# Value products of two attention steps issued together, from the start of the attention loop

## The chip, the core and the metric

The kernel runs on one core of a Trainium2 chip. The metric is the device time of one execution in microseconds (us). TensorE (PE, with its weight loads shown as PEld) multiplies matrices into PSUM, which has eight banks of 128 x 512 float32; ScalarE (ACT), VectorE (DVE) and GpSimd (POOL) work on tiles; SyncE (SP) issues DMAs. Each engine takes its instructions in the order in which the program lists them, and waits on semaphores of the others.

## The reference, cut to what matters

Two mixing layers over the same sequence length are added with a gate. The attention part, which the change touches, is a full softmax attention with 32 heads of 16 columns over 2048 positions:

```python
H = 32; Dh = D // H                      # D = 512, S = 2048
q, k, v = qkv[0], qkv[1], qkv[2]         # from x @ wqkv
scores = jnp.einsum("bhqd,bhkd->bhqk", q, k) * scale
p = _softmax(scores, axis=-1)
o = jnp.einsum("bhqk,bhkd->bhqd", p, v)
a = o.transpose(0, 2, 1, 3).reshape(B, S, D) @ wo
...
y = einsum("ts,bse->bte", dft_seq_re, a_) - einsum("ts,bse->bte", dft_seq_im, b_)
return g * a + (1 - g) * y
```

The other part multiplies with large Fourier matrices. Here it matters only because its products fill PE in the later part of the attention loop.

## The kernel before, in words

The 32 heads are 16 pairs (`NP`). For each pair the kernel needs the largest score of each query before it can take exponentials. It gets these from **scans**: a scan (`scan`, L126) multiplies 128 queries of both heads with 512 keys into one pair of PSUM banks, and one DVE reduction (L137) takes the maximum of each row. There are 64 scans to a head pair, 1024 in all. The first 725 are done beside the projections and the Fourier products, in an earlier phase; the other 299 are done one per step in the attention loop.

The **attention loop** (L991) has 512 steps. A step takes one head pair `p`, one half `h` of the queries (1024 of them) and one block `kb` of 128 keys; 16 steps make a half pass, 32 a head pair. A step issues on PE, in this order:

1. the wide scores (`qk_both`, L229): 512 queries of both heads, two matmuls into a pair of banks. ACT takes one wide exponential of 128 x 1024 (L234) into the tile `eb`;
2. a scan (`next_scan`, L979), while there are any left;
3. the narrow scores (`qk_single`, L237): the other 512 queries of both heads, into two of three single banks. ACT takes two narrow exponentials of 128 x 512 (L242) into the tiles `e`;
4. value products (`flush`, L974, which calls `pv`, L753): four matmuls of 128 x 17 by 512 columns for each step flushed, one to each 32-column strip of the array, which add into the accumulator bank `pvb`. The 17th column of the values is one, so that it sums the exponentials.

All score matmuls, the scans among them, have a contraction over at most 50 rows and come in twos, one head in the upper and one in the lower half of the array.

The list `pend` holds the steps whose exponentials are ordered but whose value products are not. Step 0 is appended, step 1 flushes it, and from then on the number that is flushed in a step is set by the line that the change touches (L1030).

The program is placed by hand: the order written is the order on each engine. PSUM is full: the scans have one pair of banks (`wide0`), the wide scores another (`wide1`), the narrow scores the three banks d0, d1 and k0 in turn, the accumulator the bank k1. In SBUF the wide exponentials have a ring of four tiles, the narrow ones rings of three and four.

When the last key block of a half pass has been flushed (`done[2] == NB - 1`), DVE copies the accumulator to `ob` (`quotients`, L762) and GpSimd fetches the sums from it; ten steps later `divide` (L771) takes reciprocals and scales. Queries and keys of the next pair are loaded by SP at fixed steps.

`MIX` is 301, the first step without a scan. From it on each step issues three pairs of matmuls of the Fourier part or the output product (`next(fill)`), ahead of the wide scores in even steps and between wide and narrow scores in odd ones, and value products are flushed two steps at a time, in even steps.

Of the kernel before, what the change touches and what calls it, by code (L numbers as in the profile page):

```python
# [46 lines left out]
MIX = TOTAL - FRONT + 1  # L47
# [6 lines left out]
def build(tc, xT, wqkv, wo, wrT, wiT, cr, ci, gate, out):  # L54
    nc = tc.nc
    with ExitStack() as ctx:
# [51 lines left out]
        def load_use(p):  # L108
            if p < NP:
                used[p], loads = row_loads(p, nc.sync)  # L110
                for load in loads:
                    load()
                qs, ks = used[p]
                for j in range(2):
                    b = 64 * j + 48
                    nc.sync.dma_start(ks[b:b + 2, :].bitcast(F32), ones_d)
                    for n in range(2):
                        nc.sync.dma_start(qs[b + n:b + n + 1, :].bitcast(F32),
                                          m_d[p][n:n + 1, :, j].rearrange("n g b k -> n b g k"))
# [610 lines left out]
        with ExitStack() as pa:  # L730
# [15 lines left out]
            def qk2(p, h, kb, c):  # L746
                if c == 0:
                    return qk_both(p, h, kb)
                n = turn1[0]
                turn1[0] += 1  # L750
                return qk_single(p, h, kb, [ring[n % len(ring)] for ring in single])
# [10 lines left out]
            def quotients(p, h):  # L762
                ob = ap.tile([P, 512], F32, tag="ob", name="ob", bufs=2)
                nc.vector.tensor_copy(ob, pvb)  # L764
                lc = sm.tile([P, 16], F32, tag="lc", name="lc")
                for n, (c, j, r) in enumerate(quads):
                    nc.gpsimd.dma_start(lc[32 * n:32 * n + 32, :],  # L767
                                        ob[r + DH:r + VC, :].rearrange("p (s e) -> p s e", e=16))
                return p, h, ob, lc

            def divide(p, h, ob, lc):  # L771

                nc.vector.reciprocal(lc, lc)  # L773
                nc.gpsimd.dma_start(r_d[p][h].rearrange("n (s e) -> (n s) e", e=16), lc)  # L774
                for n, (c, j, r) in enumerate(quads):
                    nc.gpsimd.dma_start(rb[r:r + DH, :], r_d[p][h][n:n + 1, :].to_broadcast([DH, 512]))
                nc.gpsimd.tensor_mul(ob, ob, rb)
                kept = p >= NP - 2
                if p == NP - 2:
                    oh, ol = block(28 + 2 * h), block(29 + 2 * h)  # L780
                else:
                    pool, *tags = (cw, "chi", "clo") if kept else (ap, "oh", "ol")
                    oh, ol = (pool.tile([P, 512], F32R, tag=tag, name=tag) for tag in tags)
                nc.gpsimd.tensor_copy(oh, ob)
                nc.gpsimd.tensor_sub(ol, ob, oh.bitcast(F32))
                if kept:
                    direct.setdefault(h, []).append((oh, ol))
                    return
                for i, s in enumerate((oh, ol)):
                    nc.gpsimd.dma_start(o_d[p // 4][i][h, :, p % 4], s.bitcast(F32))  # L790
# [38 lines left out]
            def output_rows(c):  # L829

                for f in range(ND - 1):
                    for i in range(2):
                        a = oc[c, f, i] = block((0, 18)[c % 2] + 2 * f + i)
                        src = o_d[f][i][c // 2, c % 2].rearrange("p (j r) s -> r (p j) s", j=2)
                        nc.sync.dma_start(a.bitcast(F32), src[0:DH])
# [10 lines left out]
            def load_y(c):  # L846
                y4 = stk.tile([P, 4, D], F32, tag="stk", name="y4")
                nc.sync.dma_start(y4, y_d[c])
                for t in range(4 * c, 4 * c + 4):
                    ys[t] = y4[:, t % 4, :]  # L850
# [8 lines left out]
            def load_unit():  # L859
                if units:  # L860
                    t, u = units.pop(0)
                    raw = ap.tile([P, D], F32, tag="craw", name="craw", bufs=2)
                    raws.append(raw.rearrange("p (c q) -> p c q", q=P))
                    nc.sync.dma_start(raws[-1], ci[t, :, u * CS:(u + 1) * CS, :])

            def split_unit():
                if raws:
                    raw = raws.pop(0)
                    hi, lo = (cw.tile([P, 512], F32R, tag=tag, name=tag).rearrange("p (c q) -> p c q", q=P)
                              for tag in ("chi", "clo"))  # L870
                    nc.vector.tensor_copy(hi, raw)  # L871
                    nc.vector.tensor_sub(lo, raw, hi.bitcast(F32))
                    parts.append((hi, lo))
# [85 lines left out]
            def part(t, *ks):  # L959

                if t not in groups:
                    if t in (3, 9):
                        ps = pair_banks()
                        groups[t] = ps[:, 0, :], ps[:, 1, :]
                    else:
                        groups[t] = bank2() if t == 8 else (bank(), pvb if t == 11 else bank())
                for k in ks:
                    mix_rest(t, groups[t], k, k == 0 or 7 < t < 11, k == 2)
# [3 lines left out]
            halves, halved, pend = [], [], []  # L972

            def flush():  # L974
                done = pend.pop(0)
                pv(*done)
                return done

            def next_scan():  # L979
                n = seen[0]  # L980
                if n >= TOTAL:
                    return
                if n % SCANS == SCANS - 10:
                    load_scan(n // SCANS + 1)
                scan(n, pair_banks())
                seen[0] += 1
                if seen[0] % SCANS == 0:
                    late.extend(shift(n // SCANS))

            late = []  # L990
            for step in range(NP * PERIODS):  # L991
                p, i = step // PERIODS, step % PERIODS
                h, kb = i // NB, i % NB
                now[0] = step
                if i == 18:
                    load_use(p + 1)
                if step in (MIX - 24, MIX - 20):
                    load_unit()
                if step == MIX - 12:
                    split_unit()  # L1000
                if OUT - 10 <= step < OUT - 4 or step >= OUT + 4:
                    next(operands, None)
                if step in (OUT - 12, OUT + 1):
                    output_rows(int(step > OUT))
                if step in (OUT - 25, (NP - 1) * PERIODS):
                    for c in range(2):
                        load_y(c + 2 * (step > OUT))
                if step >= MIX and step % 2 == 0:
                    next(fill)
                if step == 0:  # L1010
                    pend.append((p, h, kb, ahead[:2]))
                    continue
                es = ahead[2:] if step == 1 else [qk2(p, h, kb, 0)]
                if step == 1:
                    es.append(qk2(p, h, kb, 1))
                    flush()
                if late:
                    late.pop(0)()
                if step == 2:
                    es.append(qk2(p, h, kb, 1))  # L1020
                if step > 1:
                    next_scan()
                if step > 2:
                    es.append(qk2(p, h, kb, 1))
                if step >= MIX and step % 2:
                    next(fill)
                if step == NP * PERIODS - 1:
                    part(3, 0)
                done = None
                for _ in range(min(len(pend), 1) if step < MIX else 0 if step % 2 else 2):  # L1030
                    done = flush()
                if done and done[2] == NB - 1:
                    halved.append((step + (10 if done[0] < NP - 2 else 7 if done[0] < NP - 1 else 3), quotients(*done[:2])))
                if halved and halved[0][0] <= step:
                    p_, h_ = halved[0][1][:2]
                    divide(*halved.pop(0)[1])
                    if p_ == NP - 2:
                        output_rest(h_)
                pend.append((p, h, kb, es))
# [76 lines left out]
```

## Time and profile before

| what | value |
|---|---|
| median of three runs | 1726.87 us (1726.72 to 1727.06) |
| span of the profiled execution | 1725.2 us |
| instructions | 36082 |
| chain that ended last, by engine | PE 96%, DVE 2%, DMA 1%, issue 1% |
| chain, largest lines | value products L755 29%, Fourier and projection products L185 25%, attention scores L210 19% |
| granted TensorE clock, 40 slices | 9 tenths or more in every slice |
| wide exponential of step 3 begins | 670.9 us |
| wide exponential of step 301 begins | 1237.1 us |

The profiled execution has no time of its own beside its span. In the rows below, a line number is that of the listing. A row of a group names the line, the engine, the operation, the output tile and the inputs, the shapes and the count, then the busy time and the mean duration in ns of one, then the idle time of the engine ahead of them and what ended it. A row of the order of time begins with start and duration in us; neighbours of one kind are merged, and a bracket at the end holds the idle time ahead and what ended it. All value products are at L755, wide and narrow scores at L210, scans at L135. The ends of matmuls are modelled, so that a busy PE can be a waiting one; its weight loads carry the semaphore waits.

### The profile page before, as it was taken

Reading aid. Unit: us, or ns where it says so; the run is one execution under the profiler, and the core shown is the slowest. Engines: PE = TensorE matmul, PEld = TensorE weight load, DVE = VectorE, ACT = ScalarE, POOL = GpSimd, SP = SyncE. Lnnn points to the kernel's source line nnn. Section 1 sums busy time; section 2 is a strip of 40 time slices with the busy share of each in tenths; the row PEclk is TensorE's granted clock in tenths of the full one; section 3 lists DMA queues with packets and bytes.
Section 4 is the critical chain, followed back from the end, with each engine's and each line's share of the span. In section 5 each row is a group of like instructions: output and inputs, shape, how many; then the busy total and the mean of one; then the engine's idle time right before and its main releaser. Section 6 shows DMA issues by size and latency. Waiting matters only on the chain.

```text
span 1725.2 us, 36082 instructions
## 1 busy us (share of the span) xinstructions
PE 1713.5 (99%) x13680; PEld 1044.7 (61%) x13680; DVE 1089.1 (63%) x2059; ACT 1506.8 (87%) x2489; POOL 648.7 (38%) x770
## 2 busy tenths in 40 slices
PE   9999999999999999999999999999999999999998
PEld 7888888988888885333333333333455555555554
DVE  6898888999999996666666666666512212122333
ACT  6447889888888888999999999999988888888886
POOL 3672436655555762223233242322322322223222
PEclk9999999999999999999999999999999999999999
DMA  7783557534337663243323342351334244265712
GB/s 257 241 285 75 156 158 211 158 112 115 103 111 211 153 136 72 37 73 58 66 59 67 54 82 44 58 107 37 65 80 94 72 110 91 67 150 139 175 36 101
DMA packets 123710, 193.03 MB, mean 112 GB/s; under 512 B 54112, under 2 KB 56656, under 8 KB 116624
## 3 DMA queue, kind: packets, MB, share of 16 engines
q1 hardware_dynamic: 84464, 170.20, 37.7%
q0 software_dynamic: 38496, 19.47, 5.7%
q8 instruction: 107, 1.75, 0.4%
q10 hardware_dynamic: 576, 1.05, 0.2%
q14 instruction: 67, 0.55, 0.1%
HBM read 129.63 MB, written 61.61 MB: 111 GB/s over the span
## 4 chain that ended last, share of the span: by engine, by line
PE 96%; DVE 2%; DMA 1%; issue 1%; ACT 0%; SPq 0%; DVEq 0%; POOL 0%; ACTq 0%; POOLq 0%
PE pvb L755 29%; PE xy L185 25%; PE s L210 19%; PE s L185 9%; PE s L154 9%; PE s L135 5%; DVE fold L160 1%; DMA q_d<-eh 0%; DMA raws<-wqkv 0%; DMA ks<-kf_d 0%; PE s L554 0%; DVE y L853 0%; ACT fold L158 0%; DVE s L278 0%; DVE b L334 0%
## 5 line engine op out<-in xcount | busy, mean ns | idle before, releaser
L234 ACT ACTIVATE eb<-s 128x1024 f32<-128x1024 f32 x512 | 578.7, 1130 | 65.4 <-PE s L210 65.4
L242 ACT ACTIVATE e<-s 128x512 f32<-128x512 f32 x1022 | 608.9, 709 | 0.4 <-PE s L210 0.4
L137 DVE TENSOR_REDUCE mx<-s 128x2 f32<-128x1024 f32 x364 | 441.4, 1224 | 188.7 <-PE s L135 188.5
L755 PE MATMUL pvb<-eb,va 128*17 128x512 f32 x2052 | 513.0, 597 | 0.0
L755 PE MATMUL pvb<-e,va 128*17 128x512 f32 x2044 | 512.1, 597 | 0.0
L160 DVE CUSTOM_DVE_ANT_0 fold<-s,fold 128x512 f32<-128x512 f32 x660 | 443.9, 690 | 52.7 <-PE s L154 24.4
L158 ACT ACTIVATE fold<-s 128x512 f32<-128x512 f32 x660 | 389.9, 603 | 73.3 <-PE s L154 52.3
L210 PEld LDWEIGHTS s<-qs,ks 50*128 50x128 f32 x2048 | 214.9, 184 | 355.2 <-ACT eb L234 255.1
L210 PE MATMUL s<-qs,ks 50*128 50x512 f32 x2048 | 420.0, 434 | 0.0
L185 PE MATMUL xy<-b,c 64*128 64x512 f32 x2448 | 397.3, 392 | 0.3 <-ACT c L333 0.3
L154 PE MATMUL s<-ks,qs 48*128 48x512 f32 x1320 | 315.3, 405 | 1.6 <-DVE mx L160 1.0
L185 PEld LDWEIGHTS xy<-b,c 64*128 64x128 f32 x2448 | 283.9, 187 | 17.6 <-issue 1.0
L154 PEld LDWEIGHTS s<-ks,qs 48*128 48x128 f32 x1320 | 172.9, 184 | 47.0 <-DVE mx L160 12.5
L774 POOL DMA_DIRECT2D r_d<-lc x31 | 18.1, 583 | 456.4 <-DVE lc L773 456.4
L755 PEld LDWEIGHTS pvb<-eb,va 128*17 128x17 f32 x2052 | 70.5, 96 | 189.9 <-issue 182.7
L135 PE MATMUL s<-ks,qs 48*128 48x512 f32 x728 | 151.6, 394 | 0.7 <-DVE mx L137 0.7
L767 POOL DMA_DIRECT2D lc<-ob x124 | 62.9, 514 | 156.3 <-DVE ob L764 156.1
L185 PE MATMUL xy<-w,b 64*128 64x512 f32 x768 | 115.3, 392 | 0.0
L365 POOL TENSOR_TENSOR c<-craw,c 128x512 fp32r<-128x512 f32 x84 | 109.4, 1302 | 6.7
L185 PE MATMUL s<-b,chi 64*128 64x512 f32 x670 | 105.4, 391 | 0.0
L364 POOL CAST c<-craw 128x512 fp32r<-128x512 f32 x84 | 53.3, 635 | 125.1 <-PE xy L185 120.1
L871 DVE CAST chi<-craw 128x512 fp32r<-128x512 f32 x40 | 19.1, 477 | 111.4 <-PE s L185 99.3
(136 smaller groups left out, 1535.2 us busy)
## 6 DMA issues: line engine op xcount, KB each, us to landing
qs<-q_d SPq DMA_DIRECT2D x66, 256.0 KB
craw<-ci SPq DMA_DIRECT2D x64, 256.0 KB
craw<-cr SPq DMA_DIRECT2D x60, 256.0 KB
ks<-k_d SPq DMA_DIRECT2D x44, 256.0 KB
qs<-q_d SPq DMA_DIRECT2D x66, 128.0 KB
ab_d<-ab SPq DMA_DIRECT2D x32, 256.0 KB
y_d<-y SPq DMA_DIRECT2D x32, 256.0 KB
o_d<-oh POOLq DMA_DIRECT2D x28, 256.0 KB, 13.8
```

Of the source, the lines that this page charges most:

```text
L135: nc.tensor.matmul(ps[:, j, :], qs[b:b + 48, qb * P:(qb + 1) * P], ks[b:b + 48, c * 512:(c + 1) * 512], start=True, stop=True)
L137: nc.vector.tensor_reduce(mx[p][:, :, qb, c], ps, axis=AX.X, op=ALU.max)
L154: nc.tensor.matmul(ps, qs[b:b + 48, qb * P:(qb + 1) * P], ks[b:b + 48, c * 512:(c + 1) * 512], start=True, stop=True)
L158: nc.scalar.activation(fold[j], ps, AF.Relu)
L160: nc.vector.tensor_tensor_reduce(out=fold[j], in0=ps, in1=fold[j], scale=1.0, scalar=-3.0e38, op0=ALU.add, op1=ALU.max, accum_out=mx[p][:, ...
L185: nc.tensor.matmul(ps[j], lhs[r], rhs[r], start=first, stop=last)
L210: nc.tensor.matmul(pss[j], ks[b:b + 50, kb * P:(kb + 1) * P], qs[b:b + 50, q0:q0 + 512], start=True, stop=True)
L234: nc.scalar.activation(e, ps, AF.Exp, scale=SCALE)
L242: nc.scalar.activation(e[j], pss[j], AF.Exp, scale=SCALE)
L365: sub(lo, raw, hi.bitcast(F32))
L755: nc.tensor.matmul(pvb[r:r + VC, :], va[:, kb, 2 * p + j, :], es[c][j], start=kb == 0, stop=kb == NB - 1, tile_position=(0, r))
L767: nc.gpsimd.dma_start(lc[32 * n:32 * n + 32, :], ob[r + DH:r + VC, :].rearrange("p (s e) -> p s e", e=16))
```

## The change

The number of steps flushed no longer depends on the phase. Before, each step under 301 flushed one step if there was one; now odd steps flush none and even steps up to two, in the whole loop.

```diff
                 done = None
-                for _ in range(min(len(pend), 1) if step < MIX else 0 if step % 2 else 2):
+                for _ in range(0 if step % 2 else min(len(pend), 2)):
                     done = flush()
                 if done and done[2] == NB - 1:
```

Step 2 still flushes step 1 alone. From step 4 on, an even step flushes the two steps before it: step 4 flushes 2 and 3, step 300 flushes 298 and 299. The last key block of a half pass has an odd step number and was flushed in the even step behind it; it still is.

## The prediction

> **What bounds the kernel now.** I read the page's totals first, then the totals of two stretches (the attention loop with scans, and the loop after them), the groups of instructions of the first stretch, and last the order of time inside single steps.
>
> ```profile
> PE 1713.5 (99%) x13680; PEld 1044.7 (61%) x13680; DVE 1089.1 (63%) x2059; ACT 1506.8 (87%) x2489; POOL 648.7 (38%) x770
> ```
>
> ```profile
> 670.90:1237.00 566.10, 565.38 (x4174) 215.91 (x4176) 383.27 (x354) 565.38 (x895) 164.53 (x249) 1.00 0.33 61
> 1241.50:1650.00 408.50, 408.50 (x3351) 215.58 (x3349) 91.55 (x154) 360.60 (x554) 106.71 (x160) 1.00 0.46 110
> ```
>
> ```profile
> L242 ACT ACTIVATE e<-s 128x512 f32<-128x512 f32 x597 | 376.0, 776 | 0.4 <-PE s L210 0.4
> L234 ACT ACTIVATE eb<-s 128x1024 f32<-128x1024 f32 x298 | 357.4, 1199 | 0.3 <-PE s L210 0.3
> ...
> L137 DVE TENSOR_REDUCE mx<-s 128x2 f32<-128x1024 f32 x298 | 365.2, 1225 | 181.3 <-PE s L135 181.3
> L764 DVE COPY ob<-pvb 128x512 f32<-128x512 f32 x18 | 12.5, 692 | 1.5
> ```
>
> The columns of the stretches are the stretch, its length, the busy time of PE, PEld, DVE, ACT and POOL, the granted clock, the DMA share and GB/s. The first stretch runs from the start of step 3's wide exponential to that of step 301's: 298 steps in 566.1 us, **1.90 us a step, 3.80 a pair**. Its 298 wide exponentials and 298 reductions confirm the count. PE and ACT are both busy throughout and DVE has gaps, so busy shares don't say which one sets the step. One step in order of time does:
>
> ```profile
> 1003.10 1.23 DVE L137 TENSOR_REDUCE mx<-s 128x2 f32<-128x1024 f32 x1 [0.69 <-PE s L135]
> 1003.22 0.10 PEld L755 LDWEIGHTS pvb<-eb,va 128*17 128x17 f32 x2 [0.37 <-issue]
> ...
> 1004.20 0.19 PEld L210 LDWEIGHTS s<-qs,ks 50*128 50x128 f32 x2 [0.85 <-ACT eb L234]
> ...
> 1004.38 0.19 PEld L135 LDWEIGHTS s<-ks,qs 48*128 48x128 f32 x2
> ...
> 1004.54 0.40 PE L135 MATMUL s<-ks,qs 48*128 48x512 f32 x2
> ...
> 1004.74 1.17 ACT L234 ACTIVATE eb<-s 128x1024 f32<-128x1024 f32 x1
> 1004.77 0.39 PE L210 MATMUL s<-qs,ks 50*128 50x512 f32 x2
> 1004.98 1.23 DVE L137 TENSOR_REDUCE mx<-s 128x2 f32<-128x1024 f32 x1 [0.65 <-PE s L135]
> 1005.09 0.10 PEld L755 LDWEIGHTS pvb<-eb,va 128*17 128x17 f32 x2 [0.36 <-issue]
> ```
>
> The scan's weights load (L135, 1004.38) 0.05 us after the previous reduction ended (1003.10 + 1.23 = 1004.33). The scan has one pair of PSUM banks, so scan n may not start before reduction n-1 has left it. From scan load to reduction start is 0.60 (1004.38 to 1004.98), the reduction takes 1.23, the release 0.05: a ring of 1.88 us through PE and DVE, which is the step. DVE's "idle" 0.65 lies inside that ring, and the 0.85 in the row at 1004.20 is PEld's pause while PE runs products; the exponential it names had ended before. What a late reduction costs, one step shows, where other DVE work stood ahead of it:
>
> ```profile
> 1214.74 1.22 DVE L137 TENSOR_REDUCE mx<-s 128x2 f32<-128x1024 f32 x1
> 1214.79 0.18 PEld L210 LDWEIGHTS s<-qs,ks 50*128 50x128 f32 x2 [0.85 <-ACT eb L234]
> ...
> 1215.34 1.10 ACT L234 ACTIVATE eb<-s 128x1024 f32<-128x1024 f32 x1
> 1216.01 0.19 PEld L135 LDWEIGHTS s<-ks,qs 48*128 48x128 f32 x2 [1.03 <-DVE mx L137]
> ...
> 1216.68 0.10 PEld L755 LDWEIGHTS pvb<-eb,va 128*17 128x17 f32 x2 [0.37 <-issue]
> ...
> 1218.20 1.02 ACT L234 ACTIVATE eb<-s 128x1024 f32<-128x1024 f32 x1 [0.30 <-PE s L210]
> ```
>
> The reduction ended at 1215.96, the scan's load followed at 1216.01, everything behind it on PE came later by as much, and this step took 2.86 us (1215.34 to 1218.20).
>
> **The change part by part.** In steps 3 to 300 the order on PE becomes: odd step: wide scores, scan, narrow scores; even step: the same three, then the value products of the last two steps. No instruction is added or removed, and no DMA, scan, division or copy of the accumulator changes its step: the last product of a half pass already comes in an even step. So the count of busy work is the same, and the cost is one of order alone. The exponentials are kept a step longer; the rings of 4, 3 and 4 buffers hold that without a wait, since the narrow one of step n needs the products of n-3, which are issued by step n-1 in either parity. Price: nothing.
>
> (a) The scans lose their even spacing. Between the scan of an even step and the next stands the whole double group of products; between the scan of an odd step and the next stand only narrow and wide scores, which are short, so PE arrives at the second scan while DVE still reads the first. The loop after the scans already issues products in pairs and shows the length of a double group:
>
> ```profile
> 1398.98 1.03 ACT L234 ACTIVATE eb<-s 128x1024 f32<-128x1024 f32 x1 [0.47 <-PE s L210]
> ...
> 1400.85 1.04 ACT L234 ACTIVATE eb<-s 128x1024 f32<-128x1024 f32 x1
> ...
> 1400.97 0.10 PEld L755 LDWEIGHTS pvb<-eb,va 128*17 128x17 f32 x2 [0.24 <-issue]
> ...
> 1402.81 0.30 PEld L210 LDWEIGHTS s<-qs,ks 50*128 50x128 f32 x4 [0.85 <-ACT e L242]
> ```
>
> I follow the new pair from the odd step's wide-score load at 0:
> - load to reduction start 0.78 (1004.20 to 1004.98);
> - reduction 1.23;
> - release to the even step's scan load 0.05, so that load stands at 2.06;
> - late scan load to first product load 0.67 (1216.01 to 1216.68, the row with the same kind of delay; 0.71 from 1004.38 to 1005.09 without it);
> - double group to the next odd wide-score load 1.84 (1400.97 to 1402.81).
>
> Sum **4.57 us a pair** against 3.80: 0.77 more. There are 298/2 = 149 pairs, so 149 x 0.77 = 114.7 us.
>
> (b) Is the reduction really the last to arrive in the even step? Its rival there is the odd step's wide exponential, which frees the other bank pair. It starts 0.54 after the load (1004.20 to 1004.74), lasts 1.03 when ACT is not backed up (1398.98), and the release, shortest here, is this:
>
> ```profile
> 870.00 1.24 ACT L234 ACTIVATE eb<-s 128x1024 f32<-128x1024 f32 x1
> ...
> 871.35 0.19 PEld L210 LDWEIGHTS s<-qs,ks 50*128 50x128 f32 x2 [0.85 <-ACT eb L234]
> ```
>
> 0.11. So the even wide scores load at 1.68, and the scan behind them could load some 0.18 later, at 1.86; it waits to 2.06. Queued behind that wait on PE are the even narrow scores, the double group and the odd wide scores, for which ACT waits next.
>
> (c) The saving the grouping can bring is one entry into the products and one return from them per pair. Two single groups take 2 x 0.98 (1003.22 to 1004.20), a double one 1.84: 0.12 saved; entering costs 0.32 (1004.77 to 1005.09) where two neighbouring score groups stand 0.23 apart (1004.54 to 1004.77): 0.09 more; the first score group after a return needs 0.34 to the next (1004.20 to 1004.54), again 0.11 over 0.23. These 0.32 are already in the sum, since it uses the double group and only one entry; they fall into time that PE spends waiting. The Trainium skill, TensorEngine Tiling (Array Packing), section Tiling Modes, says that changing the tiling mode drains TensorE, which speaks for fewer changes; these rows agree with it in kind, and by that rule alone the sum would be that of the first rival below.
>
> (d) Ends of the unknown terms. The accumulator's copy (692 ns, x18) comes between the last product of a half pass and the odd reduction. It can start about when the odd load does, and the reduction is 0.78 behind that, so I take 0; exposed in full it is 18 x 0.69 = 12.5 us. The entry of 0.71 in place of 0.67 adds 149 x 0.04 = 6. On the low side, if the reduction were not the last, the pair is 0.54 + 1.03 + 0.11 + 0.89 (1004.20 to 1005.09) + 1.84 = 4.41, 91 us more than now instead of 115.
>
> The profiled span is 1725.2 us and the median of the runs 1726.87, so 1.7 us lie around the span or between executions. 1725.2 + 114.7 + 1.7 = **1841.6 us**.
>
> **The rivals.**
> First, on the other side: PE's own work is the bound, and the even scan does not have to wait. Then a pair is six score groups and one double group: 0.34 + 4 x 0.23 to the sixth, 0.32 to the products, 1.84: 3.42 us, or 57 us less, 1670. ACT stops that short: wide to wide exponential without a gap is 1.87 (1398.98 to 1400.85), 3.74 a pair, 9 us less, 1718. It decides from the point where the odd reduction ends before the even scan reaches PE, that is if 0.78 + 1.23 + 0.05 were below about 0.34 + 0.23 + 0.23, or the scan had a second bank pair. For it: PE is busy 565.38 of 566.10 us. Against it: the 0.05 us between reduction and scan load, and the step at 1216. 2 in 100.
>
> Second, the exponential alone sets the pair, 4.41: 149 x 0.61 = 91, 1818 us. For it: 1.68 and 2.06 lie close, and a shorter way from scan to reduction would do. Against it: the late load in the quoted step came exactly 0.05 after the reduction. 10 in 100.
>
> Third, a further wait in series: exposed accumulator copies, the slower entry, and an odd narrow exponential that frees its bank late for the even narrow scores. The first two are 12.5 + 6 us; the third I bound by the wait already in the sum, 2.06 - 1.86 = 0.20 a pair, 30 us. Together 1890 us at most; half of it, 1866, is the value I give it. 8 in 100.
>
> Fourth, the gaps on PE make the granted clock fall. Each pair has 4.57 - 3.42 = 1.15 us of them. At half clock the terms that PE sets, 0.78 + 0.67 + 1.84, double: 7.86 a pair, 149 x 4.06 = 605, 2332 us. Against it: the clock stays 1.00 over the stretch that holds the 1.03 us wait. 1 in 100. The Trainium skill, TensorE: Matmul & The Clock Gate, section A second HAM failure mode: psum-queue depth-cycling, describes a kernel whose short idles between groups of matmuls made the clock oscillate; no row here shows such a fall.
>
> Fifth, nothing measurable: the first stretch stays at 3.80 because ACT is the bound before and after and its queue covers the double group. Against it: after a double group ACT is idle 0.47 (1398.98), and there it has no scan in front of its next scores. 1727 us, 2 in 100.
>
> **How the numbers follow.** The forecast has the remaining 77 in 100; its own range is 1828 to 1858 (4.48 to 4.68 a pair). Taking in the exponential alone and half of the third rival gives 1814 to 1866. About 3.5 us (0.2%) is what a measurement here tells from no change: faster 0.02 (first), same 0.02 (fifth), slower 0.96.
>
> **What would show it.** In the changed profile: wide exponentials at two alternating distances, about 2.7 and 1.87 us, sum 4.57; "PEld s L135 <- DVE mx L137" near 0.2 to 0.4 us in 149 even steps; the even scan's load 0.05 after the odd reduction's end; 1.84 from first product load to the next score load; ACT idle some 0.8 us a pair ahead of the odd wide exponential; the loop after step 301 as now. I am wrong if the even scan's load does not wait for DVE, if the pair is under 4.4 or over 4.7 us, or if the clock in the first stretch is under 1.00.

## The result, and the profile after

The changed kernel takes **1844.0 us** (median of 4 runs, 1843.34 to 1844.43) against 1726.92 us before: ratio 1.0676, 95% interval 1.0661 to 1.0692, 117 us slower. The forecast was 1841.6. The profiled span grew from 1725.2 to 1842.4 us.

The stretch from step 3's wide exponential to that of step 301, from the totals by stretch of the changed kernel (columns as above), then two groups and three waits of that stretch (a wait's columns are the idle time in all, its count and the longest, in us):

```profile
670.71:1354.32 683.61, 586.58 (x4174) 201.88 (x4174) 384.50 (x355) 581.04 (x895) 165.01 (x249) 1.00 0.26 51
```

```profile
L242 ACT ACTIVATE e<-s 128x512 f32<-128x512 f32 x597 | 328.3, 616 | 0.8 <-PE s L210 0.8
L234 ACT ACTIVATE eb<-s 128x1024 f32<-128x1024 f32 x298 | 308.1, 1034 | 101.1 <-PE s L210 101.1
```

```profile
PEld s L210 <- ACT eb L234: 161.7, 149, 1.1
...
PE s L210 <- ACT eb L234: 96.0, 149, 0.7
PEld s L135 <- DVE mx L137: 37.3, 140, 1.3
```

The stretch took 683.6 us where it took 566.1: all of the 117 us are here. From step 301 to the end both kernels need 488.1 us (1842.4 - 1354.3, 1725.2 - 1237.1). PE is no longer busy throughout (586.6 of 683.6), and ACT has 101 us of idle ahead of wide exponentials, 0.68 a pair. They idle in turn, PE while it waits for exponentials and ACT while PE runs the double group, which is what a ring of waits looks like: by the profile no moment of the stretch has both idle, and 96.0 of PE's 97.0 us stand ahead of the even wide scores. The weight loads of scans wait for DVE 140 times, 0.27 us each on average.

One pair in order of time, an odd step and the even step behind it:

```profile
1003.83 0.19 PEld L210 LDWEIGHTS s<-qs,ks 50*128 50x128 f32 x2 [0.85 <-ACT e L242]
...
1004.38 1.02 ACT L234 ACTIVATE eb<-s 128x1024 f32<-128x1024 f32 x1 [0.66 <-PE s L210]
...
1004.62 1.23 DVE L137 TENSOR_REDUCE mx<-s 128x2 f32<-128x1024 f32 x1 [1.51 <-PE s L135]
...
1005.46 0.18 PEld L210 LDWEIGHTS s<-qs,ks 50*128 50x128 f32 x2 [1.09 <-ACT eb L234]
...
1005.89 0.19 PEld L135 LDWEIGHTS s<-ks,qs 48*128 48x128 f32 x2 [0.25 <-DVE mx L137]
...
1006.00 0.19 PEld L210 LDWEIGHTS s<-qs,ks 50*128 50x128 f32 x2
...
1006.57 0.10 PEld L755 LDWEIGHTS pvb<-eb,va 128*17 128x17 f32 x2 [0.37 <-issue]
...
1008.41 0.19 PEld L210 LDWEIGHTS s<-qs,ks 50*128 50x128 f32 x2 [0.85 <-ACT e L242]
```

The terms can be read off: odd load to reduction 0.79, reduction 1.23, its end (1005.85) to the even scan's load 0.04, scan load to products 0.68, products to the next odd load 1.84. Together 4.58, the distance of the two odd loads.

One pair stands out. Around step 289 a split of other data on DVE made the odd reduction late, and the clock fell after it:

```profile
1326.83 0.18 PEld L135 LDWEIGHTS s<-ks,qs 48*128 48x128 f32 x2 [1.34 <-DVE mx L137]
...
1327.86 0.11 PEld L755 LDWEIGHTS pvb<-eb,va 128*17 128x17 f32 x2 [0.65 <-issue]
...
1330.94 0.19 PEld L210 LDWEIGHTS s<-qs,ks 50*128 50x128 f32 x2 [1.22 <-issue]
```

```profile
1323.59:1327.00 3.41, 1.75 (x14) 0.84 (x12) 2.85 (x4) 2.77 (x4) 2.03 (x4) 1.00 0.32 87
1327.00:1330.41 3.41, 3.41 (x18) 0.71 (x20) 1.23 (x1) 1.23 (x3) 0.00 (x0) 0.50 0.33 104
```

The double group took 3.08 us (1327.86 to 1330.94) where it takes 1.84, at a granted clock of 0.50 over 3.41 us. The same pair took 4.80 us in the kernel before, at full clock.

### The profile page after: what moved, and what is told of

It is laid out like the page before. It is cut to its first block, busy times and chain, and to the rows that moved or that the text cites. A ratio compares the mean times of both kernels' runs of the same rounds, so it can differ in the third digit from the quotient of the medians.

```text
span 1842.4 us, 36082 instructions
## 1 busy us (share of the span) xinstructions
PE 1734.8 (94%) x13680; PEld 1026.9 (56%) x13680; DVE 1090.4 (59%) x2059; ACT 1522.6 (83%) x2489; POOL 649.7 (35%) x770
## 3 DMA queue, kind: packets, MB, share of 16 engines
q8 instruction: 107, 1.75, 0.4%
## 4 chain that ended last, share of the span: by engine, by line
PE 87%; ACT 9%; DVE 2%; issue 1%; DMA 1%; SPq 0%; DVEq 0%; POOL 0%; ACTq 0%; POOLq 0%
PE pvb L755 26%; PE xy L185 23%; PE s L210 16%; PE s L185 9%; PE s L154 9%; ACT eb L234 8%; PE s L135 4%; DVE fold L160 1%; DMA q_d<-eh 0%; DMA raws<-wqkv 0%; ACT fold L158 0%; PE s L554 0%; DVE y L853 0%; DVE s L278 0%; SPq L524 0%
## 5 line engine op out<-in xcount | busy, mean ns | idle before, releaser
L234 ACT ACTIVATE eb<-s 128x1024 f32<-128x1024 f32 x512 | 529.0, 1033 | 166.9 <-PE s L210 166.9
L242 ACT ACTIVATE e<-s 128x512 f32<-128x512 f32 x1022 | 560.5, 614 | 0.8 <-PE s L210 0.8
L755 PE MATMUL pvb<-eb,va 128*17 128x512 f32 x2052 | 487.2, 596 | 0.0
L755 PE MATMUL pvb<-e,va 128*17 128x512 f32 x2044 | 486.4, 596 | 0.0
L210 PEld LDWEIGHTS s<-qs,ks 50*128 50x128 f32 x2048 | 199.3, 185 | 396.8 <-ACT e L242 217.1
L154 PE MATMUL s<-ks,qs 48*128 48x512 f32 x1320 | 315.4, 405 | 1.6 <-DVE mx L160 1.0
L755 PEld LDWEIGHTS pvb<-eb,va 128*17 128x17 f32 x2052 | 84.0, 97 | 242.9 <-issue 242.6
L154 PEld LDWEIGHTS s<-ks,qs 48*128 48x128 f32 x1320 | 172.7, 184 | 46.8 <-DVE mx L160 12.5
L135 PE MATMUL s<-ks,qs 48*128 48x512 f32 x728 | 166.2, 437 | 1.2 <-DVE mx L137 1.0
L135 PEld LDWEIGHTS s<-ks,qs 48*128 48x128 f32 x728 | 72.7, 185 | 42.2 <-DVE mx L137 38.1
```

Source lines behind the costliest of these rows:

```text
L135: nc.tensor.matmul(ps[:, j, :], qs[b:b + 48, qb * P:(qb + 1) * P], ks[b:b + 48, c * 512:(c + 1) * 512], start=True, stop=True)
L154: nc.tensor.matmul(ps, qs[b:b + 48, qb * P:(qb + 1) * P], ks[b:b + 48, c * 512:(c + 1) * 512], start=True, stop=True)
L210: nc.tensor.matmul(pss[j], ks[b:b + 50, kb * P:(kb + 1) * P], qs[b:b + 50, q0:q0 + 512], start=True, stop=True)
L234: nc.scalar.activation(e, ps, AF.Exp, scale=SCALE)
L242: nc.scalar.activation(e[j], pss[j], AF.Exp, scale=SCALE)
L755: nc.tensor.matmul(pvb[r:r + VC, :], va[:, kb, 2 * p + j, :], es[c][j], start=kb == 0, stop=kb == NB - 1, tile_position=(0, r))
```

## The experiments

Theories: **R**, the reduction of the odd step holds the even scan; **E**, the exponentials set the pair; **P**, the double group is the cost, whatever PE waits for; **N**, the narrow banks hold the even step; **A**, ACT's rate is the floor of the single order. Pairs are the distances of the odd steps' wide exponentials from step 3 to 301, 149 of them.

### Half a reduction, in both orders

```diff
-            nc.vector.tensor_reduce(mx[p][:, :, qb, c], ps, axis=AX.X, op=ALU.max)
+            seen_ = ps if n <= FRONT else ps[:, :, 0:256]
+            nc.vector.tensor_reduce(mx[p][:, :, qb, c], seen_, axis=AX.X, op=ALU.max)
```

In pairs:

> Products in pairs, and each reduction of the attention loop reads only the first 256 of the 512 scores of a head, so half of the maxima's inputs are left out; the scan matmuls stay. Theory R (the odd step's reduction, which holds the scans' only bank pair, is last to arrive in the even step): the reduction falls from 1.23 to about 0.65 us, is released 0.78 + 0.65 + 0.05 = 1.48 after the odd wide-score load, and leaves the path; the next to arrive is the wide exponential (release at 1.68, pair 4.36 us) or the narrow bank that the odd step's first narrow exponential frees (release near 2.17 in the changed kernel's profile, pair about 4.45). Time 1844 - 149 x (0.12 to 0.21) = 1813 to 1826 us. Theory E (the exponentials alone set the pair, the reduction only covers them): pair stays at 4.52 or more, 1837 us or more. Theory P (the double group itself is the cost, whatever PE waits for): unchanged, 1844.

Measured: 1815.54 us (ratio to before 1.0515, 1.0496 to 1.0535), 28.5 us less than the changed kernel; the median pair is 4.38. The order of time of this kernel:

```profile
1002.87 0.18 PEld L211 LDWEIGHTS s<-qs,ks 50*128 50x128 f32 x2 [0.85 <-ACT e L243]
...
1003.41 1.02 ACT L235 ACTIVATE eb<-s 128x1024 f32<-128x1024 f32 x1 [0.48 <-PE s L211]
...
1003.65 0.69 DVE L138 TENSOR_REDUCE mx<-s 128x2 f32<-128x512 f32 x1 [1.91 <-PE s L135]
...
1004.33 1.08 ACT L243 ACTIVATE e<-s 128x512 f32<-128x512 f32 x2
1004.49 0.18 PEld L211 LDWEIGHTS s<-qs,ks 50*128 50x128 f32 x2 [1.09 <-ACT eb L235]
...
1004.60 0.19 PEld L135 LDWEIGHTS s<-ks,qs 48*128 48x128 f32 x2
...
1004.83 0.33 PEld L211 LDWEIGHTS s<-qs,ks 50*128 50x128 f32 x2
```

The reduction ends at 1004.34, before the even wide scores load at all; the scan's load follows them by 0.11 and carries no wait. Theory R holds: the reduction leaves the path, and the time falls into the range expected for that. Two waits now lie close together. The even wide scores load right behind the wide exponential (its end 1004.43, load at 1004.49); from there 0.89 + 1.84 would give a pair of 4.35. The even narrow scores come a little later: their two weight loads spread over 0.33 us where they take 0.19 in the changed kernel, since the second, at 1004.98, needs the bank of the odd step's first narrow exponential, which ends at 1004.92. That load stands 2.11 after the odd one, the products load 0.42 behind it (1005.40), and 2.11 + 0.42 + 1.84 is 4.37, so the narrow bank is what arrives last here. 0.58 of the 0.77 us that the pairing costs stay: the reduction is the last wait and not the only one.

In the order of before:

> The order of before, with the same halved reduction. If the ring through the reduction set the step of before (1.88 us), it falls to about 1.30 and the step goes to the next bound: ACT back to back 1.87 to 1.895, or PE's own round near 1.82. ACT as the next bound: 298 x (0.005 to 0.03) = 1 to 9 us faster, 1718 to 1726. PE as the next bound: 298 x 0.08 = 24 us faster, 1703. If the reduction was not the bound: within 1 us of 1727.

Measured: 1725.78 us (11 runs), ratio 0.9997 (0.9988 to 1.0005): no change, though the scan now waits for nothing. Its exponentials:

```profile
L243 ACT ACTIVATE e<-s 128x512 f32<-128x512 f32 x597 | 370.5, 757 | 0.0
L235 ACT ACTIVATE eb<-s 128x1024 f32<-128x1024 f32 x299 | 353.3, 1182 | 0.2 <-PE s L211 0.2
```

ACT is idle for 0.2 us in all, and its instructions are recorded longer (1182 and 757 ns) than in the changed kernel (1034 and 616): they overlap more, each starting 0.27 us (median) before the one ahead has ended, against 0.12 there.

### A longer reduction in odd steps, in pairs

```diff
             nc.vector.tensor_reduce(mx[p][:, :, qb, c], ps, axis=AX.X, op=ALU.max)
+            if n > FRONT and n % 2 == 0:
+                nc.vector.tensor_reduce(mx[p][:, 1, qb, c:c + 1], ps[:, 1, :], axis=AX.X, op=ALU.max)
```

The other two kernels read `ps[:, 1, 0:32]` and `ps[:, 1, 0:256]` there; the second result overwrites the first, so in these two the maximum of that head leaves out the other columns. The whole head again:

> The changed kernel with nothing left out; in odd steps of the attention loop DVE reduces one of the two heads a second time, about 0.69 us more before the bank pair is free. Theory R (nothing lies between the odd reduction's end and the even scan): all of it is paid, 149 x 0.69 = 103 us, 1947 us. Theory E or P (the even step waits for the exponentials, or the double group is the cost): at most what exceeds their 2.06 and 1.68, under half of it, 1895 us or less.

Measured: 2179.11 us, far over every expectation, with a mean granted clock of 0.895. The totals in stretches of one clock window each:

```profile
735.82:739.23 3.41, 3.37 (x16) 1.02 (x20) 1.23 (x1) 1.68 (x3) 0.00 (x0) 0.51 0.00 0
739.23:742.65 3.42, 2.13 (x16) 0.67 (x8) 1.92 (x2) 2.21 (x4) 0.00 (x0) 1.00 0.00 0
742.65:746.06 3.41, 3.26 (x26) 1.18 (x26) 1.23 (x2) 2.00 (x4) 0.00 (x0) 1.00 0.00 0
746.06:749.47 3.41, 1.99 (x16) 0.76 (x18) 2.63 (x3) 3.19 (x5) 0.00 (x0) 0.99 0.00 0
749.47:752.89 3.42, 3.42 (x20) 1.01 (x10) 0.67 (x2) 0.70 (x3) 0.80 (x2) 0.51 0.02 2
```

For most of the stretch the clock alternates between full and half in windows of 3.41 us, 132 half ones in the loop with scans. The 17 pairs that ran at full clock took 5.40 to 5.41 us, 0.84 more than the changed kernel's: theory R's size (0.69, and 0.15 of gaps and release). The others took about 7.0. So this run answers the question on R only in those 17 pairs, and raised another; two smaller doses followed.

> The changed kernel with nothing left out; in odd steps DVE reduces 32 more columns after the reduction. In the kernel that reduces a whole head again, the pairs at full clock took 5.41 us, 0.84 over the changed kernel: 0.69 for the second reduction, 0.03 between the two, 0.12 more from its release to the products. By that and about 0.19 us for 32 columns, theory R gives 0.33 a pair: 4.90 us at full clock, 149 x 0.33 = 49 us, 1893 us, if the clock holds. If the clock falls as often as there (in 133 windows of 3.41 us): 149 x 1.9 = 280 us, 2120 us or more.

Measured: 1936.0 us. The median pair is 4.89, as expected, and 26 of the 149 take 6.5 us or more, as many as there are half-clock windows. One of these (the lower row) and the window ahead of it, in the totals by stretch:

```profile
825.48:828.90 3.42, 2.50 (x19) 1.02 (x16) 2.16 (x4) 2.55 (x4) 1.89 (x4) 1.00 1.00 167
828.90:832.31 3.41, 3.41 (x18) 0.48 (x16) 1.08 (x1) 1.35 (x3) 0.14 (x1) 0.50 1.16 200
```

> As its neighbour with 256 more columns, about 0.43 us. Theory R: 0.58 a pair, 5.15 us at full clock, 149 x 0.58 = 86 us, 1930 us if the clock holds; 2140 us or more if it falls in nearly every pair. The two sizes tell between which lengths of a pair the clock begins to fall.

Measured: 1947.35 us; in the profiled execution the median pair is 5.12, and there are 19 half-clock windows. The falls differ between executions of this one program: the two took 1957.46 us (the profiled one) and 1937.25, at mean granted clocks of 0.982 and 0.992. Against the changed kernel's 4.57 the medians rise by 0.32 and 0.55 for 0.33 and 0.58 expected: theory R pays in full as long as the clock holds. E and P, which allow less than half, fall. The longer dose has fewer falls than the shorter one, so the number of falls is no simple function of the pair's length; how the pairs lie against the windows may count too, and that was not tried apart.

### The even step's scan behind its narrow scores

```diff
+                last = step > 2 and step % 2 == 0
-                if step > 1:
+                if step > 1 and not last:
                     next_scan()
                 if step > 2:
                     es.append(qk2(p, h, kb, 1))
+                if last:
+                    next_scan()
```

> Products in pairs, nothing left out; in even steps the scan stands behind the narrow scores instead of ahead of them, so that it reaches PE after the odd reduction has ended. Theory R with no other wait near: the pair is then that of the wide exponential, 0.54 + 1.03 + 0.11 + 0.84 + 1.84 = 4.36, 1813 us. Theory N (the narrow scores of the even step also wait, for the bank that the odd step's first narrow exponential leaves at about 2.17): the narrow scores now take the wait and the scan follows them; scan load 0.11 + 0.23 later, pair about 4.68, 1860 us. Theory P: unchanged, 1844.

Measured: 1849.77 us (ratio 1.0714, 1.0694 to 1.0733), median pair 4.61. Theory R alone is refuted as a full account, N stands, with a price somewhat too high:

```profile
1003.98 1.23 DVE L137 TENSOR_REDUCE mx<-s 128x2 f32<-128x1024 f32 x1 [1.28 <-PE s L135]
...
1005.30 0.18 PEld L210 LDWEIGHTS s<-qs,ks 50*128 50x128 f32 x1 [0.19 <-ACT e L242]
1005.31 0.29 PEld L135 LDWEIGHTS s<-ks,qs 48*128 48x128 f32 x2
```

The wait moved from the scan to the second narrow weight load, which needs the bank of the odd step's first narrow exponential.

### Without the scans of the loop

Four kernels leave out the loop's scans and reductions; a constant stands for those maxima. One keeps the order of before, one the pairs, one the pairs with the two free banks given to the narrow scores of odd steps (d0 and d1 serve the even ones), one the pairs with these banks given to the wide scores of odd steps.

```diff
-                scan(n, pair_banks())
+                if n % SCANS == 0:
+                    new_maxima(n // SCANS)
+                if n % SCANS == 0 or n == FRONT + 1:
+                    nc.vector.memset(mx[n // SCANS], 150.0)
```

> The order of before; the 298 scans of the loop from step 3 on, and step 2's, are left out with their reductions, and the maxima that they would give are replaced by a constant. The round of before is tied: PE alone 0.90 + 0.98 = 1.88 us, ACT back to back 1.87 to 1.895. Without the scans PE's round is about 0.23 shorter, 1.65. Theory A (the exponentials are the floor of the loop in this order): step stays at 1.87 to 1.90, 1718 to 1727 us. Theory PE (PE's round was the bound): 1.66 to 1.75 a step, 1655 to 1685 us.

> Products in pairs, the scans of the loop left out as in the other kernel. If the even scan's wait for the reduction were the only thing that the pairing costs, the pair would come to ACT's floor, 3.75 to 3.80, and the time to that of the single order without scans, 1718 to 1727. Theory E (the one wide bank pair and the three narrow banks also keep PE from working ahead): wide exponential 0.54 + 1.03 + 0.11, then two score groups and the entry 0.66, then 1.84: 4.18 us; with the narrow bank freed 2.10 after the odd load (as measured with the scan last) 2.10 + 0.44 + 1.84 = 4.38. Time 1725 + 149 x (0.38 to 0.58) = 1782 to 1812.

> As the kernel without scans and with products in pairs; the two banks that the scans leave free take the narrow scores of odd steps, and d0 and d1 those of even steps, so that narrow scores never wait for the step just before. Theory N (the narrow bank holds the even step): pair from 4.38 down to 4.18, 30 us faster than its neighbour. Theory E with the wide bank pair alone: no difference, both at 4.18.

> Products in pairs, the scans of the loop left out (their maxima replaced by a constant); the two banks that they leave free now serve the wide scores of odd steps, and the narrow ones keep their three banks. If the waits for the wide pair and for the narrow bank lie in series behind each other (each holds the even step by itself): the even narrow scores still wait for the odd step's first narrow exponential, 2.10 + 0.44 + 1.84 = 4.38 us a pair, no gain over the neighbour's 4.37, 1813 us. If the wide bank pair is what holds the pair: 4.12 or less, 1776 us.

| kernel | us | ratio to before | pair, us |
|---|---|---|---|
| single, no scans | 1726.76 | 0.9999 (0.9989 to 1.0008) | 3.79 |
| pairs, no scans | 1813.12 | 1.0497 (1.0476 to 1.0518) | 4.37 |
| pairs, no scans, four narrow banks | 1776.6 | 1.0286 (1.0265 to 1.0306) | 4.12 |
| pairs, no scans, two more wide banks | 1812.04 | 1.0492 (1.0461 to 1.0522) | 4.37 |

Theory A holds: 299 scans and reductions can go from the single order without any gain. In pairs, the narrow bank holds the even step (4.37 to 4.12 when freed), and freeing the wide pair in its place gains nothing, since the narrow wait stands behind it:

```profile
1004.55 0.18 PEld L210 LDWEIGHTS s<-qs,ks 50*128 50x128 f32 x1 [1.35 <-ACT e L243]
```

(the kernel with two more wide banks). With four narrow banks the load that waits is that of the even wide scores:

```profile
1005.26 1.02 ACT L234 ACTIVATE eb<-s 128x1024 f32<-128x1024 f32 x1 [0.22 <-PE s L210]
...
1006.34 0.30 PEld L210 LDWEIGHTS s<-qs,ks 50*128 50x128 f32 x4 [1.32 <-ACT eb L234]
```

That the last 0.33 us a pair (4.12 against 3.79) are this wait is read from the row, not shown: both relieved at once would need nine banks (four wide, four narrow, the accumulator).

### The scan ahead of the wide scores, single order

```diff
+                if step > 1:
+                    next_scan()
                 es = ahead[2:] if step == 1 else [qk2(p, h, kb, 0)]
...
-                if step > 1:
-                    next_scan()
```

> The order of before, nothing left out; the scan stands ahead of the wide scores in each step. The ring through the reduction is shorter, since the scan's load to the reduction's start is then 0.54 instead of 0.60: 0.54 + 1.23 + 0.05 = 1.82. If that ring alone set the step of before: step 1.87 (ACT), 9 us faster, 1718. If ACT's own rate set it: within 3 us of 1727. If the wide scores, now behind a possibly waiting scan, come too late for ACT: slower, by 298 x 0.1 = 30 us at most.

Measured: 1734.06 us, ratio 1.0043 (1.0029 to 1.0056), slower; the median step is 1.903. A shorter ring through the reduction buys nothing here either:

```profile
1013.18 0.19 PEld L135 LDWEIGHTS s<-ks,qs 48*128 48x128 f32 x2 [0.85 <-DVE mx L137]
...
1013.72 1.23 DVE L137 TENSOR_REDUCE mx<-s 128x2 f32<-128x1024 f32 x1 [0.67 <-PE s L135]
...
1014.07 0.12 PEld L755 LDWEIGHTS pvb<-eb,va 128*17 128x17 f32 x4 [0.27 <-issue]
...
1015.08 0.19 PEld L135 LDWEIGHTS s<-ks,qs 48*128 48x128 f32 x2 [0.85 <-DVE mx L137]
```

The reduction ends at 1014.95, 0.13 ahead of the scan's load at 1015.08, so the 0.85 in that row is again PEld's pause while PE runs products. The round on PE is 0.89 + 1.01 = 1.90 where it was 0.89 + 0.98 before, and the exponentials no longer queue (mean durations 1025 and 601 ns against 1199 and 776). No order tried beats the kernel before.

## Why the prediction was right, and where it was not

**The sum.** Its five terms came within 0.01 of the rows above (0.79, 1.23, 0.04, 0.68, 1.84 for 0.78, 1.23, 0.05, 0.67, 1.84). 683.6 / 149 is 4.588 a pair for 4.57. The excess, 149 x 0.018 = 2.7 us, is the one pair at step 289 (7.25 us), where a late reduction and a half-clock window fell together; neither was in the sum.

**The last wait** (step b) was the reduction, as said; halving it takes the pair to 4.38, and lengthening it is paid in full. That 4.38 lies near the second rival's 4.41 is in part luck: that sum took the release as 0.11, which was 0.06 here, and what arrives last with half a reduction is the narrow bank and not the wide exponential that the rival named. The exponentials alternate by 2.69 and 1.88 us for 2.7 and 1.87 forecast. ACT's idle was 0.68 a pair and not 0.8.

**The bound of before failed.** The prediction called the ring through the reduction "which is the step". The 0.05 us between reduction and scan load are real, but with half the reduction, and with none, the step stays at 1.89 to 1.90, and the kernel's time with it. Three things were tied there: that ring at 1.88, PE's round of 0.89 + 0.98, and ACT. ACT is the floor the experiments show, since it stays when the other two shrink. Its rate in a steady row of steps is 3.79 / 2 = 1.90; the 1.87 used for the first rival was the distance of two starts in a short burst. So that rival's 1718 was too low: ACT alone holds the loop at the time of before. The forecast survived because the new ring did not rest on what bounded the old one.

**The saving by grouping** (step c): the double group takes the 1.84 us that were forecast, against 2 x 0.98. That this and the saved entry fall into waiting fits the rows, but no run takes it apart.

**The third rival** named the narrow bank and bounded it without placing it. It is the wait next in line: hidden by 0.07 us in the changed kernel (the bank is free 2.10 after the odd load, as the kernel with the scan last shows, and the even narrow scores load at 2.17, 1003.83 to 1006.00) and in force as soon as the reduction is halved, or the scan moves or goes.

**The fourth rival** (1 in 100) is the one judged too lightly. In the changed kernel the clock fell once, and 0.3 us more in each pair makes it fall 26 times. A fall cost less than the rival took: 1.6 to 1.7 us for a pair (7.03 against 5.41 with a whole head more, 6.5 to 6.6 against 4.89 with 32 columns), and not the 3.29 by which the terms that PE sets would grow, since the half clock lasted one window of 3.41 us and ended inside the pair.

## What to carry to other kernels

Grouping instructions of one kind can shorten them (here 1.84 us for two groups of products against 1.96), but it spreads the work that feeds other engines unevenly. With one buffer between producer and consumer, the two uses that now stand close together run in series, and the group behind them is added on top. Before such a change, follow one period from a load to the same load through each buffer with a single copy, and take the longest; freeing one ring only uncovers the next. A wait that ends just ahead of an instruction, as the scan's 0.05 us here, can be a tie and not the bound: shorten it alone and see whether the step moves.

## What the hardware showed beside this

A half clock without a long idle. In the kernel that reduces a whole head again, the two gaps on PE in a pair are 0.62 and 0.81 us on average (92.4 / 149 and 113.9 / 141, from its waits over the loop with scans):

```profile
PE s L135 <- DVE mx L139: 113.9, 141, 1.9
PE s L212 <- ACT eb L236: 92.4, 149, 0.7
```

Yet the clock was 0.50 to 0.51 for 3.41 us behind windows in which PE was busy 1.99 of 3.41 us. With 32 more columns 2.50 of 3.42 was followed by a fall. In the changed kernel this was not:

```profile
1016.39:1019.80 3.41, 2.75 (x22) 0.99 (x16) 1.80 (x3) 2.74 (x6) 1.13 (x3) 1.00 0.02 2
```

PE's busy time is modelled, and there is no plain limit in it: the window with 2.13 of 3.42 quoted above, itself behind a half-clock one, was followed by full clock. With 256 more columns, in the totals by stretch, two full-clock windows with nearly the same PE busy time, 2.25 and 2.26, went different ways:

```profile
1292.75:1296.16 3.41, 2.25 (x20) 0.83 (x20) 2.47 (x4) 3.34 (x5) 3.27 (x4) 1.00 0.00 0
1296.16:1299.57 3.41, 2.75 (x24) 0.79 (x12) 1.99 (x4) 2.23 (x5) 1.49 (x2) 1.00 0.29 27
...
1302.99:1306.40 3.41, 2.26 (x20) 0.85 (x20) 2.69 (x4) 3.31 (x5) 2.02 (x4) 1.00 1.20 249
1306.40:1309.81 3.41, 3.41 (x20) 1.01 (x12) 0.55 (x1) 0.70 (x3) 0.00 (x0) 0.50 0.87 129
```

What decides between them stays open. What the runs show is that the changed kernel stands near the edge, where a late reduction can cost more than its own length. The Trainium skill, TensorE: Matmul & The Clock Gate, section What's actually happening, gives windows of about 3.4 us and a half rate after an idle one. The trace agrees with the length (3.41) and the rate (0.50), and differs on what counts as idle, since the windows shown ahead of the falls held PE work of 1.75 to 2.50 us.
